# Attention and token/channel mixer on one core: left-over rows multiplied side by side, one load for q and k, a new order

## The chip, the cores and the metric

The kernel runs on one core of one Trainium2 chip, as one program. Its metric is the device time of one execution in microseconds (us). The core's engines run side by side, each on its own list of instructions: TensorE (PE in the profile, with PEld for its weight loads), VectorE (DVE), ScalarE (ACT), GpSimd (POOL) and SyncE (SP). They wait for each other by semaphores. DMAs are issued from the lists of SP and of ACT.

## The reference

Eight attention heads of 576 positions and 64 channels for a batch of 4 feed two mixing layers. All numbers are float32.

```python
scores = q @ k.T / sqrt(64) + bias[head, i, j]       # bias from a small network of log1p|i-j| / log1p(i)
attn = exp(scores - max); attn = attn / (sum(attn) + 1e-9)
x = (attn @ v) laid out as (batch, 576, 512)
u = x + (relu(x.T @ w_tok1) @ w_tok2).T              # mixing over the 576 positions, 256 inner
out = u + relu(u @ w_ch1) @ w_ch2                    # mixing over the 512 channels, 1536 inner
```

## The kernel before, in words

**Precision.** TensorE multiplies in pieces: an operand is split into a high part and the left-over low part, and high x high, high x low and low x high are summed in PSUM. So every product is three matmuls. q and k are split into rounded float32 parts (`kh`, `kl`, `qh`, `ql`), the softmax numerators, v, x and the weights into float16 parts.

**Units.** A unit is one batch entry and one pair of heads; there are 16 (`unit`). The 576 query rows of a unit are four chunks of 128 rows and 64 left-over rows. In the four chunks the two heads have separate score products, each over 64 contracted rows (the two heads lie in the two halves of the partitions). The left-over rows of both heads share one score product: head 0 in partitions 0 to 63, head 1 in 64 to 127.

**Steps of a chunk.** `scores` (PE, L792) writes a pair of PSUM banks; `biased` (DVE, L801) adds the bias and takes the row maximum; `numer` (ACT, L814) takes the exponential. Then 128x128 blocks of the numerators are turned so that keys lie on partitions: by TensorE (`flip`, L843), read out as high part by ACT (L846) and low part by DVE (L849); in chunks 0, 2 and the left-over chunk three of the blocks go by a DMA transpose, after ACT (L824) and POOL (L828, then L389) made the halves. `back` (PE, L870 to L872) multiplies the turned blocks by v, 30 matmuls a chunk, five blocks for each head; an extra column of ones in v gives the row sums.

**The left-over rows in `back`.** Turned block tiles hold 128 columns, of which a head owns 64. The kernel loads 128 columns from a place shifted by 64, so that the wanted rows land in the half of the partitions that the batch entry's parity asks for; the other half comes out as rubbish. For this the turned tiles have 64 extra columns at each end, which `fillt` (L619) sets to zero at the start. Both heads' results land in the same 64 partitions, in two column ranges.

**Normalisation.** After chunks 1 and 3, and again after the left-over rows, DVE adds a guard to the row sums (`norm1`, L891), takes reciprocals (`norm2`, L895) and multiplies (`norm3`, L904): nine instructions a unit. The result is `x`, of which ACT takes the high part (`xh`) and POOL the low part (`xl`).

**Token mixing of the unit.** `mix1` (L920 to L922) and `mix2` (L929 to L931) are 30 matmuls each. The left-over 64 positions are a fifth chunk, in the half of the partitions given by the parity; the weight tile `wt1` has two versions of its last chunk, one for each parity. The sum goes to DRAM (`um`, and `ul` for the left-over rows).

**Loads.** k and q of a unit come by one DMA each, issued from ACT's list (L750), into one buffer each (`kk`, `qq`). ACT rounds each (two activations, L374); POOL takes the low parts (L389; for the first unit DVE). The rounded tiles have two buffers.

**Order.** Nothing of the order is left to the compiler. `Plan` takes each step with a cost per engine, the steps it follows, the buffers it takes and frees, and a due time, and plays them forward: it always takes, on the engine that is free first, the step that is ready with the smallest due time. The due times are the table `DUE` plus the unit's place; `ON` has the costs where a step may go to several engines. The engines then run their lists in that order. Where the plan sees PE idle for long, it adds dummy matmuls (`keep_warm`, L323). The four single PSUM banks are shared by the flips, the mixing steps and the sums of `back` (two holds a unit).

**Around the units.** Ahead of them the bias is built (L521, four groups of 32 array columns side by side; L526; written to DRAM and read back); token weights are decoded from 64-bit words on DVE, POOL and ACT (L639 to L656). After them the channel mixing runs (L1111 to L1113, L1202 to L1204, L1296 to L1298).

Of the kernel before, what the change touches and what calls it, by code (L numbers as in the profile page):

```python
# [29 lines left out]
NCH = 4  # L30
# [9 lines left out]
STAY = 1486.1  # L40
# [16 lines left out]
ON = {'dlo': {'P': 1.9},  # L57
      'dlo2': {'P': (1.9, 1923.78), 'V': (0.67, 744.69)},
      'late': {'P': (0.7, 2192.22), 'A': (0.58, 2154.6)},
      'klow': {'P': (1.5, 404.86), 'V': (0.83, 1698.46)},  # L60
      'zlow': {'P': (1.25, -2022.79), 'V': (0.6, 1951.58)},
      'twhole': {'P': (2.4, -5410.44), 'V': (1.21, -163.47)},
      'tsum': {'P': (3.0, 1980.67), 'V': (1.72, -1127.53)},
      'tlow': {'P': (2.1, 1817.8), 'V': (1.15, 2280.4)},
      'oall': {'P': (2.7, 1683.65), 'V': (1.2, 3850.72)},
      'norm': {'V': (0.35, -2113.5), 'A': (0.88, -183.64)},
      'over': {'A': 0.65, 'V': (0.72, 599.08)},
      'vh': {'P': (0.7, 5073.08), 'V': (0.4, -2032.12), 'A': (0.6, -2896.69)},
      'vl': {'P': (1.36, 4039.97)}}
DUE = {'tie': 4736.26,  # L70
       'blk': -676.16,
       'blkn': 59.25,
       'rect': -364.19,
       'bmm': -2656.99,
       'over': -2660.88,
       'put': -3571.25,
       'bl': -179.13,
       'bln': 44.73,
       'sums': 1179.41,
       'sumsn': 532.92,  # L80
       'measw': 321.39,
       'measwn': 107.97,
       'amax': 767.52,
       'scales': 78.49,
       'scalet': -2778.06,
       'scalec': -884.57,
       'fill': -1967.61,
       'fill1': 321.78,
       'tok': -1836.05,
       'tokn': -264.96,  # L90
       'dec1': -196.68,
       'dec2': 362.43,
       'dec3': -442.95,
       'dec4': 845.97,
       'dec5': -898.57,
       'load_k': -385.67,
       'load_q': -829.68,
       'split_k': -303.52,
       'first_k': 1018.99,
       'first_q': -464.55,  # L100
       'split_q': -401.35,
       'load_v': -2691.07,
       'prep_v': 4811.82,
       'prep_vh': -1580.3,
       'prep_vl': -5129.6,
       'scores': -1550.06,
       'biased': -570.84,
       'exp': -803.8,
       'hi': -461.44,
       'lo': 874.4,  # L110
       'turn': -277.35,
       'flip': -1079.29,
       'fliphi': -883.4,
       'flip2': -920.66,
       'fliplo': 433.23,
       'back': 787.76,
       'norm': -94.44,
       'mix0': -1114.2,
       'mix1': 190.17,
       'relu': -3325.99,  # L120
       'mix2': -2565.13,
       'mix2b': -87.08,
       'store': -2250.33,
       'w1': 437.81,
       'w1n': 293.74,
       'U0': 957.44,
       'U0n': -427.31,
       'U1n': -290.77,
       'U1': 808.64,
       'U2': -710.17,  # L130
       'Un': 48.66,
       'U3': 2131.25,
       'U4': -678.33,
       'u1': 2779.66,
       'u2': -237.57,
       'u3': -558.34,
       'u4': -2241.32,
       'u5': -756.44,
       'G': 3117.15,
       'G0': 1449.33,  # L140
       'G0n': 0.0,
       'g1': -1447.72,
       'g2': 796.85,
       'ur': -324.62,
       'H': 2342.06,
       'e1': 448.66,
       'e2': -2521.07,
       'e3': 10.12,
       'e4': 1249.03,
       't2': 1665.81,  # L150
       't3': -678.77,
       't4': -818.53,
       'T1': -762.26,
       'Tn': -160.17,
       'rd': 479.45,
       'urs': -341.92,
       'un': 158.68,
# [1247 lines left out]
```

## Time and profile before

| | |
|---|---|
| time, three runs | 632.61, 632.66, 633.25 us (median 632.66) |
| the profiled execution | 629.27 us, its span 627.3 us |
| granted TensorE clock | 1.0 in the whole span |
| busy share of the span | PE 97%, DVE 77%, ACT 65%, POOL 48% |
| units | from about 57 us to about 345 us, the last store at 362 us |

The span is the time from the first to the last instruction; some 2 us of the execution lie around it. A matmul's record lasts longer than the time until the next one can start, because matmuls are pipelined: 128x65 products have records of 0.19 us and start 0.03 us apart. So a busy PE is not a full PE, and starts tell more than durations. Each engine runs its list strictly in order, so a late operand holds up all that is behind.

### The profile page before, as it was taken

Reading aid. Unit: us, or ns where it says so; the run is one execution under the profiler, and the core shown is the slowest. Engines: PE = TensorE matmul, PEld = TensorE weight load, DVE = VectorE, ACT = ScalarE, POOL = GpSimd, SP = SyncE. Lnnn points to the kernel's source line nnn. Section 1 sums busy time; section 2 is a strip of 40 time slices with the busy share of each in tenths; the row PEclk is TensorE's granted clock in tenths of the full one; section 3 lists DMA queues with packets and bytes.
Section 4 is the critical chain, followed back from the end, with each engine's and each line's share of the span. In section 5 each row is a group of like instructions: output and inputs, shape, how many; then the busy total and the mean of one; then the engine's idle time right before and its main releaser. Section 6 shows DMA issues by size and latency. Waiting matters only on the chain.

```text
span 627.3 us, 18135 instructions
## 1 busy us (share of the span) xinstructions
PE 607.8 (97%) x7216; PEld 446.8 (71%) x7216; DVE 484.5 (77%) x1220; ACT 407.3 (65%) x751; POOL 302.0 (48%) x343
## 2 busy tenths in 40 slices
PE   8999988999999999999999999999999999999997
PEld 4446776898898889889889964444444468845886
DVE  7887899889999899999899969985764784355322
ACT  7998889797888998998898434633543641244210
POOL 1006788976775888898564620002335642212211
PEclk9999999999999999999999999999999999999999
DMA  8999678999988966556856999645122015400221
GB/s 306 397 378 332 182 190 214 266 259 206 228 190 245 213 150 148 136 120 170 144 104 148 188 358 238 204 137 135 34 67 71 31 35 135 101 1 0 85 86 33
DMA packets 102340, 104.54 MB, mean 167 GB/s; under 512 B 62192, under 2 KB 71920, under 8 KB 102256
## 3 DMA queue, kind: packets, MB, share of 16 engines
q1 hardware_dynamic: 92608, 82.79, 50.5%
q10 hardware_dynamic: 9648, 20.60, 11.1%
q8 instruction: 56, 0.92, 0.6%
q14 instruction: 28, 0.23, 0.1%
HBM read 68.88 MB, written 20.33 MB: 142 GB/s over the span
## 4 chain that ended last, share of the span: by engine, by line
PE 66%; DVE 11%; ACT 8%; POOL 8%; issue 4%; DMA 2%; ACTq 0%; SPq 0%; POOLq 0%; DVEq 0%
PE bank L1111 5%; PE bank L1113 5%; PE bank L1112 5%; PE pair L792 5%; PE bank L1297 4%; PE bank L1296 4%; PE bank L1298 4%; PE pair L521 4%; PE bank L843 4%; DVE z L801 4%; DVE t2a L849 3%; PE pair L1113 2%; PE bank L1202 2%; PE pair L1111 2%; PE bank L1204 2%
## 5 line engine op out<-in xcount | busy, mean ns | idle before, releaser
L814 ACT ACTIVATE z<-z,mx 128x576 f32<-128x576 f32 (+1 forms) x121 | 92.6, 778 | 10.1 <-DVE mx L801 8.8
L801 DVE CUSTOM_DVE_ANT_0 z<-pair,slots 128x576 f32<-128x576 f32 (+1 forms) x121 | 90.6, 756 | 5.2 <-PE pair L792 4.5
L849 DVE SCALAR_TENSOR_TENSOR t2a<-bank,t2a 128x384 f16<-128x384 f32 (+1 forms) x134 | 70.6, 536 | 6.3 <-ACT t2a L846 5.0
L843 PE MATMUL bank<-id,z 128*128 128x128 f32 x431 | 71.0, 283 | 2.1 <-ACT z L814 0.7
L846 ACT ACTIVATE t2a<-bank 128x384 f16<-128x384 f32 (+1 forms) x134 | 62.3, 471 | 12.2 <-PE bank L843 8.3
L792 PE MATMUL pair<-kh,qh 64*128 64x288 f32 (+1 forms) x288 | 61.6, 345 | 4.1 <-DVE mx L801 3.3
L1111 PE MATMUL bank<-slots 128*128 128x512 f16 (+1 forms) x168 | 58.6, 349 | 0.0
L1113 PE MATMUL bank<-slots 128*128 128x512 f16 (+1 forms) x168 | 58.6, 349 | 0.0
L1112 PE MATMUL bank<-slots 128*128 128x512 f16 (+1 forms) x168 | 58.6, 349 | 0.0
L1307 DVE SCALAR_TENSOR_TENSOR slots<-bank,crow,slots 128x256 f32<-128x256 f32 x42 | 19.6, 481 | 47.6 <-PE bank L1298 34.1
L843 PEld LDWEIGHTS bank<-id,z 128*128 128x128 f32 x431 | 45.6, 141 | 12.3 <-DVE t2a L849 3.5
L870 PE MATMUL bank<-vh,t2a 128*128 128x65 f16 x472 | 53.5, 194 | 0.0
L871 PE MATMUL bank<-vl,t2a 128*128 128x64 f16 x472 | 53.2, 191 | 0.0
L872 PE MATMUL bank<-vh,t2a 128*128 128x65 f16 x472 | 53.2, 192 | 0.0
L792 PE MATMUL pair<-kl,qh 64*128 64x288 f32 (+1 forms) x288 | 51.9, 298 | 0.0
L792 PE MATMUL pair<-kh,ql 64*128 64x288 f32 (+1 forms) x288 | 50.4, 291 | 0.0
L1241 POOL TENSOR_TENSOR me<-me 128x512 f32<-128x512 f16 x12 | 13.7, 1154 | 68.8 <-DVE wd L1087 68.4
L792 PEld LDWEIGHTS pair<-kh,qh 64*128 64x128 f32 (+1 forms) x288 | 33.9, 184 | 16.0 <-issue 7.6
L871 PEld LDWEIGHTS <-t2a 128*128 128x128 f16 x472 | 43.6, 98 | 0.2
L870 PEld LDWEIGHTS <-t2a 128*128 128x128 f16 x472 | 43.4, 97 | 0.2
L872 PEld LDWEIGHTS <-t2a 128*128 128x128 f16 x472 | 43.5, 97 | 0.0
L870 PE MATMUL bank<-vh,rect 128*128 128x65 f16 x328 | 40.9, 195 | 2.3 <-DMA rect<-rect 1.5
(272 smaller groups left out, 2100.7 us busy)
## 6 DMA issues: line engine op xcount, KB each, us to landing
keep<-wc SPq DMA_DIRECT2D x24, 512.0 KB, 4.5
wd<-wc SPq DMA_DIRECT2D x24, 512.0 KB, 4.7
bd<-slots SPq DMA_DIRECT2D x36, 295.5 KB, 6.8
slots<-bd SPq DMA_DIRECT2D x16, 576.0 KB, 7.2
tv<-v ACTq DMA_DIRECT2D x16, 320.0 KB, 3.7
qq<-qT ACTq DMA_DIRECT2D x16, 320.0 KB, 3.7
kk<-kT ACTq DMA_DIRECT2D x16, 320.0 KB, 5.0
z<-vr SPq DMA_DIRECT2D x8, 576.0 KB, 7.7
```

The costliest lines, as they stand in the source:

```text
L792: PE.matmul(out=pairs[both[h].i][:, 512 - i + n * i:512 + n * i], lhsT=qx[x][w, c * 128:c * 128 + 128], rhs=kx[y][w, k0:k0 + i], start=(j ...
L801: V.tensor_tensor_reduce(out=st["z"][z.i][:, o], in0=pairs[ph.i][:, 512 - i:512 + i], in1=bias_m[hp][:, c, h, :] if c < NCH else bias_l[hp ...
L814: A.activation(out=zz, in_=zz, func=ACTF.Exp, bias=mx_t[z.i][:, h:h + 1], scale=-1.0)
L843: PE.transpose(banks[tb.i][:, n * 128:(n + 1) * 128], st["z"][z.i][:, 384 * i + n * 128:384 * i + (n + 1) * 128], id32)
L846: A.activation(out=block(h.i, 0, m), in_=banks[tb.i][:, 0:128 * m], func=ACTF.Copy, scale=P_SCALE)
L849: V.scalar_tensor_tensor(out=block(h.i, 3, m), in0=banks[tb.i][:, 0:128 * m], scalar=P_SCALE, in1=block(h.i, 0, m), op0=ALU.mult, op1=ALU. ...
L870: PE.matmul(out=o, lhsT=lh, rhs=vh[:, n, 0:D + 1], start=(i == 0), stop=False)
L871: PE.matmul(out=ps[:, h, 0:D], lhsT=lh, rhs=vl[:, n, :], start=False, stop=False)
L872: PE.matmul(out=o, lhsT=ll, rhs=vh[:, n, 0:D + 1], start=False, stop=(i == 4))
L1111: PE.matmul(out=ps, lhsT=w[0][:, c], rhs=uh[:, c], start=(c == 0), stop=False)
L1112: PE.matmul(out=ps, lhsT=w[0][:, c], rhs=ul[:, c], start=False, stop=False)
L1113: PE.matmul(out=ps, lhsT=w[1][:, c], rhs=uh[:, c], start=False, stop=(c == 3))
```

## The change

The left-over rows of the two heads are multiplied by v in two halves of the array's columns: head 0's 64 columns write partitions 0 to 63, head 1's write 64 to 127, one after the other in turn. The zero margins of the turned tiles, the shift by parity and the second version of the weights' last chunk go; `x` holds head 0's left-over rows in the upper left and head 1's in the lower right, zeros elsewhere; the last 64 columns of `wt2` are copied once so that the second product gives both halves. `norm1` and `norm2` run after chunk 1 (four columns) and after the left-over rows (five columns); the left-over rows are multiplied in two instructions of 64 rows (`norm4`). k and q come in one DMA and are rounded by one activation; the low parts stay two. The left-over store is two DMAs. `ON` gets an entry by which the low part for the DMA transpose could go to DVE (the built program never uses it). All due times have new values.

```diff
-STAY = 1486.1
+STAY = 1932.68
-       'back': 787.76,
+       'back': 1188.32,
-                 "kk": 1, "qq": 1, "kh": 2, "qh": 2, "tv": 1, ...
+                 "kq": 1, "gh": 2, "tv": 1, ...
-    tok = [(wt1[:, 0:2], 512), (wt1[:, 2:4], 512), (wt1[:, 4:6], 512),
+    tok = [(wt1[:, 0:2], 512), (wt1[:, 2:4], 512), (wt1[:, 4:5], 256),
-        fillt = add({"P": 2.6}, DUE["fill1"], lambda e: [G.memset(t[:, a:a + 64], 0.0) for t in st["t2a"] + st["t2d"] for a in (0, 832)], after=[drawn])
+        twice = add({"P": 0.6}, DUE["tok"] + DUE["tokn"] * 6, lambda e: [copy("P", w[:, :, S:640], w[:, :, 512:S]) for w in st["w2"]], after=wt_s[3:])
-            lk = add(wire("k", 1.06), t0 + DUE["load_k"], load("kk", hk, kT), after=early, take=[hk])
-            lq = add(wire("q", 1.06), t0 + DUE["load_q"], load("qq", hq, qT), after=early, take=[hq])
+            lk = add(wire("k", 2.0), t0 + DUE["load_k"], lambda e: ENG[e].dma_start(out=st["kq"][hk.i], in_=kq[order_of[u]]), after=early, take=[hk])
-                s = add({"A": 0.63}, t0 + DUE["split_" + nm], high(o, ho, x, hx), after=[ld], take=[ho])
+            high = add({"A": 1.18}, t0 + DUE["split_k"], lambda e: copy(e, st["gh"][gk.i][0], st["kq"][hk.i]), after=[lk], take=[gk])
...
-                            d = 64 * (h - b % 2) if c == NCH else 0
-                            lh, ll = (tt[t][:, y[t] + d:y[t] + d + 128] for y in (th, tl))
+                    if c < NCH:
+                        turns = [[(h, n + h, n, slice(0, 128), i)] for h in range(2) for i, n in enumerate(range(4 * h, 4 * h + 5))]
+                    else:
+                        turns = [[(0, n + 5 * h, n, slice(64 * h, 64 * h + 64), n) for h in range(2)] for n in range(5)]
+                    for turn in turns:
+                        for x, y, d in ((th, vh, D + 1), (th, vl, D), (tl, vh, D + 1)):
+                            for h, n, t, w, i in turn:
+                                PE.matmul(out=ps[w, h, 0:d], lhsT=tt[t][:, x[t] + w.start:x[t] + w.stop], rhs=y[:, n, 0:d], ...)
...
-                if c in (0, 2):
+                if c not in (1, NCH):
                     continue
+                hr, n = Hold("rc"), 4 if c == 1 else 5
+                main = norm3 if n == 4 else lambda e, f=norm3: f(e, c=2)
+                def norm4(e, hb=hb, hr=hr):
+                    for h in range(2):
+                        q = slice(64 * h, 64 * h + 64)
+                        xo, ps, rc = st["x"][xh_.i][q, 4, q], av_of(hb)[q, 2, 0, 0:D], rc_t[hr.i][q, 2, 0]
+                        ...
+                            V.tensor_scalar(out=xo, in0=ps, scalar1=rc, scalar2=None, op0=ALU.mult)
...
-                add(wire("store", 0.07), t + DUE["store"], lambda e: ENG[e].dma_start(out=u_l[b // 2][r, cs], in_=x()[r, 5]), after=[s8], free=[xh_])]
+                *(add(wire("store", 0.05), t + DUE["store"], lambda e, q=slice(64 * h, 64 * h + 64): ENG[e].dma_start(
+                    out=u_l[b // 2][r, hp * 128 + q.start:hp * 128 + q.stop], in_=x()[q, 5, q]), after=[s8], free=[xh_]) for h in range(2))]
```

On PE, the start of the left-over rows of the first unit, of before and then of the changed kernel. `rect` is a tile turned by DMA, `vh` and `vl` are the parts of v, and the numbers behind a name tell buffers apart.

```order
L843 MATMUL bank_66<-id_73,z_122 128x128 x3
L870 LDWEIGHTS rect
L870 MATMUL bank_68<-vh_111,rect 128x65
L871 LDWEIGHTS rect
L871 MATMUL bank_68<-vl_112,rect 128x64
L872 LDWEIGHTS rect
L872 MATMUL bank_68<-vh_111,rect 128x65
```

```order
L846 MATMUL bank_69<-id_73,z_116 128x128 x3
L874 LDWEIGHTS rect
L874 MATMUL bank_67<-vh_106,rect 64x65
L874 LDWEIGHTS rect
L874 MATMUL bank_67<-vh_106,rect 64x65
L874 LDWEIGHTS rect
L874 MATMUL bank_67<-vl_107,rect 64x64
L874 LDWEIGHTS rect
L874 MATMUL bank_67<-vl_107,rect 64x64
```

Thirty loads and thirty matmuls stay thirty; each now has 64 output rows instead of 128, and neighbours belong to the two heads.

On DVE, the end of a unit in the middle of the program, of before and of the changed kernel. `rc` holds the reciprocals, `x` the unit's result, `t2a` a turned tile.

```order
L895 RECIPROCAL rc_144<-rc_144 128x4
L849 SCALAR_TENSOR_TENSOR rect<-bank_69,rect 128x384
L801 ISA z_119,mx_138<-pair_64,slots 128x576
L801 ISA mx_138 128x1
L904 TENSOR_TENSOR x_85<-bank_67,rc_144 128x256
L801 ISA z_119,mx_138<-pair_65,slots 128x576
L801 ISA mx_138 128x1
L891 TENSOR_SCALAR rc_145<-bank_67 64x2
L849 SCALAR_TENSOR_TENSOR t2a_91<-bank_66,t2a_91 128x384
L895 RECIPROCAL rc_145<-rc_145 64x2
L904 TENSOR_TENSOR x_85<-bank_67,rc_145 64x128
```

```order
L885 TENSOR_SCALAR rc_139<-bank_66 128x5
L852 SCALAR_TENSOR_TENSOR rect<-bank_69,rect 128x384
L852 SCALAR_TENSOR_TENSOR t2a_91<-bank_68,t2a_91 128x384
L888 RECIPROCAL rc_139<-rc_139 128x5
L898 TENSOR_TENSOR x_83<-bank_66,rc_139 128x256
L912 TENSOR_SCALAR x_83<-bank_66,rc_139 64x64 x2
L852 SCALAR_TENSOR_TENSOR t2a_92<-bank_69,t2a_92 128x384
```

The 128x256 multiplication of chunks 2 and 3 stood ahead of the left-over rows' sums; it now stands behind them, with two 64x64 multiplications after it.

On ACT, the rounding of q and k of a unit in the middle, of before (k is rounded 18 rows further down) and of the changed kernel:

```order
L846 ACTIVATE t2a_90<-bank_67 128x384
L374 ACTIVATE qh_105<-qq 128x640
L814 ACTIVATE z_120<-z_120,mx_139 128x576
L374 ACTIVATE xh<-x_83 128x640
L824 ACTIVATE rect<-z_120 128x384
```

```order
L814 ACTIVATE z_113<-z_113,mx_132 128x576
L375 ACTIVATE kqh_102<-kq 128x1280
L945 ACTIVATE hh<-bank_68 128x256
L849 ACTIVATE t2a_94<-bank_66 128x384
L824 ACTIVATE rect<-z_113 128x384
```

One activation of 1280 columns stands where one of 640 stood, and the second one further down is gone.

## Rows read from the trace of the kernel before

**Rows 1.** The page: the span, busy time by engine, and the last chain's shares.

```profile
span 627.3 us, 18135 instructions
PE 607.8 (97%) x7216; PEld 446.8 (71%) x7216; DVE 484.5 (77%) x1220; ACT 407.3 (65%) x751; POOL 302.0 (48%) x343
...
PE 66%; DVE 11%; ACT 8%; POOL 8%; issue 4%; DMA 2%; ACTq 0%; SPq 0%; POOLq 0%; DVEq 0%
```

**Rows 2.** Windows: stretch, length, each engine's busy time, clock, DMA share, GB/s.

```profile
57.00:137.00 80.00, 72.64 (x1074) 63.16 (x1075) 73.62 (x206) 69.86 (x132) 64.93 (x100) 1.00 0.82 219
...
57.00:345.00 288.00, 276.35 (x4593) 247.30 (x4594) 264.83 (x726) 252.85 (x476) 217.41 (x261) 1.00 0.78 185
```

**Rows 3.** A window after the units, same columns.

```profile
380.00:420.00 40.00, 40.00 (x188) 18.21 (x187) 38.83 (x80) 23.30 (x37) 0.00 (x0) 1.00 0.69 184
```

**Rows 4.** Timeline of PE, one unit's left-over rows: first and next; then scores' start.

```profile
195.88 0.19 PE L870 MATMUL bank<-vh,rect 128*128 128x65 f16 x1
...
196.79 0.52 PE L843 MATMUL bank<-id,rect 128*128 128x128 f32 x3
...
200.39 0.19 PE L872 MATMUL bank<-vh,t2a 128*128 128x65 f16 x1
200.52 0.40 PE L792 MATMUL pair<-kh,qh 64*128 64x288 f32 x2
```

**Rows 5.** Narrow and wide arrays: timeline (PE, PEld), one group's mean between.

```profile
15.67 0.57 PE L521 MATMUL pair<-rect,slots 128*32 128x464 f32 x4
...
L521 PE MATMUL pair<-rect,slots 128*32 128x464 f32 x8 | 1.0, 552 | 0.0
...
5.96 0.21 PEld L521 LDWEIGHTS pair<-slots 128*32 128x32 f32 x12 [0.27 <-DVE slots L499]
...
341.45 0.31 PEld L843 LDWEIGHTS bank<-id,z 128*128 128x128 f32 x3 [0.17 <-DVE rect L849]
```

**Rows 6.** One line of the kernel: counts, then duration min/median/max in ns.

```profile
L374 ACT ACTIVATE qh<-qq x16: 720/736/762, 20.7 to 303.5; 128x640 fp32r<-128x640 f32 x16
L374 ACT ACTIVATE me<-me x6: 1056/1057/1057, 443.4 to 505.6; 128x1024 f16<-128x1024 f32 x6
L750 ACTq DMA_DIRECT2D qq<-qT x16: 334/335/370, 10.0 to 287.0; - x16
...
L951 SPq DMA_DIRECT2D ul<-x x16: 461/482/1569, 119.0 to 362.3; - x16
```

**Rows 7.** DVE groups by shape, 140 to 300 us: busy us, mean ns.

```profile
L904 DVE TENSOR_TENSOR x<-bank,rc 128x256 f32<-128x256 f32 x19 | 8.0, 420 | 0.3
...
L904 DVE TENSOR_TENSOR x<-bank,rc 64x128 f32<-64x128 f32 x9 | 2.6, 287 | 0.2
L895 DVE RECIPROCAL rc<-rc 64x2 f32<-64x2 f32 x9 | 1.4, 159 | 0.3
L891 DVE TENSOR_SCALAR rc<-bank 64x2 f32<-64x2 f32 x9 | 1.4, 153 | 0.2
```

**Rows 8.** The last chain's pieces on POOL at the units' start: start, us.

```profile
59.27 1.02 POOL t2a L619 x12
...
60.33 0.81 POOL rect L619 x9
...
106.69 1.09 POOL wt1l L389
```

**Rows 9.** DMA issues: KB each, median us to landing.

```profile
kk<-kT ACTq DMA_DIRECT2D x16, 320.0 KB, 5.0
...
z<-vr SPq DMA_DIRECT2D x8, 576.0 KB, 7.7
```

**Rows 10.** A wait in 60 to 345 us: total us, times, longest.

```profile
ACT xh L374 <- DVE x L904: 1.4, 6, 0.4
```

**Rows 11.** POOL groups by shape: busy us, mean ns.

```profile
L389 POOL TENSOR_TENSOR kl<-kk,kh 128x640 fp32r<-128x640 f32 x15 | 23.3, 1555 | 2.8 <-ACT kh L374 0.8 <-ACT z L814 0.7 <-issue 0.7
...
L647 POOL TENSOR_TENSOR keep<-keep 128x512 f32<-128x512 f32 x12 | 14.0, 1165 | 10.6 <-DVE keep L644 9.7 <-ACT t2a L846 1.0
```

More of the change, by code (lines that the diff above doesn't have):

```diff
@@ L70 @@
[L70 to L115, printed above, removed]
-       'back': 787.76,
[L117 to L157, printed above, removed]
-       'v1': 443.15,
-       'v2': 3631.75,
-       'v3': 1579.05,
-       'v4': 3836.34,
-       'v5': 958.72,
-       'v6': 674.78,
-       'v7': 160.67,
-       'v8': -1837.21,
-       'w2m': -1548.46,
-       'w2mn': 106.13}
@@ L690, in attention_mixer @@
         wt_s, plain_s = [], []
[L691 removed]
+        places = [slots[:, 3, 3674 + 512 * i:3674 + 512 * i + (512, 512, 256)[i]] for i in range(3)]
         places += [slots[:, 2, 8 * S + 288 * i:8 * S + 288 * i + 288] for i in range(2)] + [slots[:, 1, 8 * S + 288 * i:8 * S + 288 * i + 288] for i in range(2)]
@@ L874, in unit @@
-                backs.append(chain("back", add({"T": 0.917}, t + DUE["back"], back, after=[*turned_s, v3, *set_ok, *backs[-1:]], take=[hb, xh_] if c == 0 else [hb] if c == 2 else [],
+                    if c < NCH:
+                        turns = [[(h, n + h, n, slice(0, 128), i)] for h in range(2) for i, n in enumerate(range(4 * h, 4 * h + 5))]
+                    else:
+                        turns = [[(0, n + 5 * h, n, slice(64 * h, 64 * h + 64), n) for h in range(2)] for n in range(5)]
@@ new lines, in back @@
+                    for turn in turns:
+                        for x, y, d in ((th, vh, D + 1), (th, vl, D), (tl, vh, D + 1)):
+                            for h, n, t, w, i in turn:
+                                PE.matmul(out=ps[w, h, 0:d], lhsT=tt[t][:, x[t] + w.start:x[t] + w.stop], rhs=y[:, n, 0:d],
+                                          start=(i == 0 and x is th and y is vh), stop=(i == 4 and x is tl))
+                backs.append(chain("back", add({"T": 0.917 if c < NCH else 0.52}, t + DUE["back"], back, after=[*turned_s, v3, *set_ok, *backs[-1:]], take=[hb, xh_] if c == 0 else [hb] if c == 2 else [],
@@ L941, in unit @@
                 out=st["hh"][1], in0=p1(), scalar=0.0, in1=st["hh"][0], op0=ALU.max, op1=ALU.subtract), after=[s4], use=[b1])
-            s6 = chain("mix", add({"T": 1.7}, t + DUE["mix2"], mix2, after=[s5, *wt_s[3:]], take=[b2], free=[hh], use=[b1]))
+            s6 = chain("mix", add({"T": 1.7}, t + DUE["mix2"], mix2, after=[s5, *wt_s[3:], twice], take=[b2], free=[hh], use=[b1]))
             s7 = add({"V": 0.67}, t + DUE["mix2b"], lambda e: V.scalar_tensor_tensor(
```

253 lines of the change are left out of this document (169 added, 84 removed).

## The prediction

> **What bounds the kernel now.** I read the page's busy shares and its last chain first [rows 1], then windows by stage [rows 2, 3], then the lines that the change touches. The page calls PE 97% busy, which says little. After the units PE is busy 40 of 40 us, and the change gives it no less to do there [rows 3]; so what can move is the part up to about 343 us. The chain spends 66% of 627.3 us on PE, that is 414 us, of which some 284 lie after 343; 130 are left, 38% of the first 343 us. The 11% of DVE are 69 us, the 8% of ACT and of POOL 50 us each, nearly all of it ahead of 343: about 20%, 15% and 15% [rows 1]. In the units' stretch DVE is busy 265 of 288 us, ACT 253 without the time in which it issues DMAs, PE 276 by its long records [rows 2]. So no engine alone is the bound: the chain changes hands, and of a microsecond taken from one engine about its share of the chain should come through. I use 0.38 for PE, 0.20 for DVE, 0.15 for ACT. It is an estimate: an engine freed alone gives less, all freed together give more.
>
> **The left-over products (PE).** The thirty matmuls of a unit run from 195.88 to 196.79 us: 0.91 us, 30 ns from start to start, with nothing waiting in between [rows 4]. After the change they are fifteen pairs. Does the array run two column halves side by side? The bias stage answers for four groups of 32 columns: one 464-column matmul has a record of 0.55 us, and four of them, one for each group, took 0.57 us together [rows 5]. So streaming takes 15 x 30 ns = 0.46 us. The loads are less sure. The only loads of narrow arrays in the trace, twelve of 32 columns, took 0.21 us; one takes 0.11, so they follow each other 9 ns apart [rows 5]; twice as many columns would be 18 ns, and thirty loads 0.55 us. At the pace of full-width float32 loads, three in 0.31 us with 0.14 for one [from the same row: (0.31 - 0.14) / 2 = 85 ns for 128 columns], 64 columns would be 43 ns, and thirty in a row 1.28 us. I take 0.55, since that row is of column groups. Changing how the array is cut costs about 0.10: scores on two row halves start 0.13 us after the last product, against 0.03 otherwise [rows 4]. Together 0.65, bounds 0.46 and 1.48 (two changes). So 0.26 less a unit, between 0.45 less and 0.57 more; by sixteen units and 0.38: **-1.6 us**, bounds -2.7 and +3.5.
>
> The Trainium skill has a rule against this part. "TensorEngine Tiling (Array Packing)", section Tiling Modes, says that column tiling switches off fast weight load, and "TensorE: Matmul & The Clock Gate", section LDWEIGHTS, gives a load without it columns/1.2 ns. By that a 64-column load is an estimated 53 ns: 0.80 us for fifteen pairs side by side, 1.6 us in a row, and the term would be about 0 or +4.8 us. No run so far shows a float16 load of 64 columns.
>
> **q and k (ACT).** Two activations of 640 columns take 0.736 us each; 1024 columns take 1.057, so 0.84 ns a column, and 1280 columns 1.27 [rows 6]. That is 0.20 less; one DMA issue of 0.335 goes as well [rows 6]. 0.53 a unit, x 16 x 0.15: **-1.3 us**. The bounds are 0, if ACT only waits longer, and -8.5, if ACT were the bound throughout. Behind the long activation stand exponentials and read-outs, which may be 0.5 us later; that is the reason to stay at the chain's share. The DMA now brings 640 KB; the nearest row, 576 KB, lands after 7.7 us, against 5.0 for 320 KB [rows 9]. Nobody feels it while the loop of the one buffer fits a unit: 0.34 issue + 7.7 + 1.27 + two low parts of 1.56 on POOL [rows 11] = 12.4 us, against 288/16 = 18 us a unit. The cover is 5.6 us; without it scores of every unit would be late by the rest. The second left-over store costs SP 0.48 us a unit [rows 6]; a DMA transpose may stand behind it, but DMA is 2% of the chain [rows 1], so between 0 and 0.2 us: nothing.
>
> **Normalisation (DVE).** The group of the left-over rows goes: 153 + 159 + 287 ns = 0.60 us; a fifth column in the sums is counted at nothing, since with two columns these instructions already take 0.15 us. Two multiplications of 64x64 come: not shown; each is at least the 0.15 of a tiny tensor_scalar that reads PSUM and at most the 0.29 of 64x128 [rows 7]. I take 0.20, nearer to the tiny one, as half the 64x128's columns. So 0.20 less a unit, between 0.30 and 0.02; x 16 x 0.20: **-0.6 us**, bounds -4.8 (DVE the bound) and 0.
>
> **The start (POOL).** The memsets of the margins stand in the chain at 59 to 61 us with 1.02 + 0.81 us [rows 8]; they go. The third token part halves: of its POOL work the joining product, 1.17 us at full size [rows 11], and the last low part, 1.09 in the chain [rows 8], give back 0.55 each. The new copies of 64 columns come behind the last low part of the second weights, and the first unit's `mix2` now waits for them; between 0.2 us (two of the memsets) and 1.09, say 0.4. Net 2.5 us. DVE is busy 73.6 of 80 us in that stretch and POOL 64.9 [rows 2], so DVE is soon the next; I count two thirds: **-1.6 us**, bounds 0 and -2.5.
>
> **Sum.** -1.6 - 1.3 - 0.6 - 1.6 = -5.1 us. The profiled execution took 629.27 us, 2 us more than its span, so it would be 624.2. It is 3.4 us (0.5%) below the median of the runs shown; the same amount off the median 632.66 gives **627.6 us**. The new order is counted at nothing in this sum: on the places shown it only makes room for the new instructions.
>
> **Rivals.**
> *Narrow loads in a row.* Thirty loads of 64 columns, one after the other at the pace of float32 loads, hold a left-over group at 1.28 + 0.10 = 1.38 us: 0.47 more a unit, x 16 x 0.38 = +2.9; with the other -3.5 the sum is -0.6, **632.0 us**. For it: the only fast 30 ns pace in the trace is that of full 128-column loads [rows 4]. Against it: the 9 ns of the 32-column ones [rows 5]. The Trainium skill's rule above would, with loads in a row, put this case near 634, an estimate by its page's figure.
>
> *The unit's end gets longer (slower).* The multiplication of chunks 2 and 3 now stands behind the left-over rows' sums, and the bank that holds both stays taken until two more instructions are done. Before, 0.60 us of DVE lay between the last product and `x`; after, 0.15 + 0.16 + 0.42 + 2 x 0.20 = 1.13 [rows 7]. ACT's high part of `x`, POOL's low part, `mix1` and the next taker of the bank all wait that 0.53 us more. If it comes through in every unit, 8.5 us: -5.1 + 8.5 = +3.4, **636.0 us**. It decides from ten units of sixteen on (5.1/0.53). For it: ACT already waits for just this multiplication, 6 times in the units [rows 10]. Against it: only 1.4 us in all, 0.4 at the longest; mixing of a unit runs beside the next unit's scores.
>
> *The new order frees more.* In 57 to 137 us PE lacks 80 - 72.6 = 7.4 us even by its long records [rows 2], for POOL's and DVE's work comes late there. If the shorter start lets the first units close up and half of that goes, -3.7 more: **623.9 us**. For it: all due times are new. Against: DVE has 6.4 us of room there and no more.
>
> **Chances.** The sum as it stands 0.56; narrow loads in a row 0.12; the longer end 0.12; a freer order 0.20. The likeliest is 627.6, by itself between 624.5 and 630.5. The range takes in the freer order with ACT or PE nearer to the bound than its chain share (two times the shares of PE and ACT, -2.9 more than 623.9, is 621.0) and most of the slow case: 620.5 to 634.5. What this measurement can tell from no change is about 0.2%, 1.3 us: faster means below 631.4, slower above 633.9. Of the first case 0.53 is faster, all of the freer order, 0.04 of the narrow loads; slower are 0.10 of the longer end and 0.03 of the narrow loads. So 0.77 faster, 0.10 the same, 0.13 slower.
>
> **What would show it.** In the changed trace: the left-over group on PE in 0.5 to 0.7 us from first to next start (right), 0.9 (no gain) or 1.3 and more (loads in a row); a rounding activation near 1.27 us; 64x64 multiplications near 0.2; units that end 3 to 5 us earlier relative to 57 us, with the stretch after them unchanged; ACT's wait for the multiplication before `xh` not above some 3 us in all. Wrong would be: PE idle behind the normalisation in most units, scores waiting for low parts of q and k, or a stretch after the units that has changed by more than a microsecond.

## The result, and the profile after

The changed kernel takes 636.1 us (median), the kernel before 632.8 beside it: a ratio of 1.0068, 95% interval 1.0053 to 1.0084. So the change is slower by 0.7%, 4.3 us, where 5.1 us less was forecast. Run once more among the experiments, it came out at 1.0055 (1.0028 to 1.0081).

The page of the changed kernel, profiled at 636.24 us: the span, the engines' busy times, the granted clock in 40 slices, and the last chain's shares.

```profile
span 634.5 us, 18086 instructions
PE 610.0 (96%) x7216; PEld 444.8 (70%) x7216; DVE 478.8 (75%) x1204; ACT 405.8 (64%) x735; POOL 297.5 (47%) x321
...
PEclk9999899999999889999999999999999999999999
...
PE 72%; DMA 7%; DVE 7%; ACT 6%; POOL 3%; issue 3%; SPq 1%; ACTq 0%; DVEq 0%; POOLq 0%
```

Against [rows 1], DVE has 6 us less to do, ACT 1.5, POOL 4.5, and yet the span is longer. DMA went from 2% of the chain to 7%, and the clock has two dips that the page of before does not have. The first of them (0.66 over 65 to 70 us) is absent in other runs of the same order and is left aside.

First the parts, on the engines where they act. The left-over rows of a unit on PE's timeline (the two columns in front are start and length), then the first scores:

```profile
161.59 0.22 PE L874 MATMUL bank<-vh,rect 128*64 128x65 f16 x2
161.64 0.20 PE L874 MATMUL bank<-vl,rect 128*64 128x64 f16 x2
...
162.06 0.20 PE L874 MATMUL bank<-vh,t2a 128*64 128x65 f16 x2
162.18 0.60 PE L792 MATMUL pair<-kqh 64*128 64x288 f32 x2
```

Fifteen pairs start 33 ns apart and 0.59 us pass until the scores, against 0.91 from the first product to the next matmul in [rows 4]. So two loads and two matmuls of 64 columns go where one of 128 went. The prediction quoted a rule of the Trainium skill against this: "TensorEngine Tiling (Array Packing)" says that column tiling switches off fast weight load (the rule stands in section Tile-to-Partition Mapping, Restrictions, not in Tiling Modes). With the estimate of 53 ns a load by the formula of "TensorE: Matmul & The Clock Gate", section LDWEIGHTS, a group would take at least 0.80 us; the measured 0.59 decides against it.

DVE's normalisation by shape in 140 to 300 us (busy us, mean ns of one, idle before), to be held against [rows 7]:

```profile
L898 DVE TENSOR_TENSOR x<-bank,rc 128x256 f32<-128x256 f32 x18 | 7.6, 421 | 0.4
L912 DVE TENSOR_SCALAR x<-bank,rc 64x64 f32<-64x64 f32 x18 | 5.0, 280 | 0.1
L888 DVE RECIPROCAL rc<-rc 128x5 f32<-128x5 f32 x9 | 1.7, 184 | 0.1
...
L885 DVE TENSOR_SCALAR rc<-bank 128x5 f32<-128x5 f32 x9 | 1.4, 159 | 5.7 <-PE bank L874 5.7
```

ACT's rounding of q and k as one, in 60 to 345 us, and the load's issues (KB each, median us to landing):

```profile
L375 ACT ACTIVATE kqh<-kq 128x1280 fp32r<-128x1280 f32 x15 | 19.0, 1267 | 0.7 <-PE pair L792 0.7
...
kq<-kq ACTq DMA_DIRECT2D x16, 640.0 KB, 5.1
```

The rounding takes 1.27 us as forecast. A 64x64 multiplication takes 0.28 us, not 0.20, so DVE saves only 0.03 us a unit.

The loss that can be seen stands near 215 us. SP's list of the changed kernel there, with the six bias loads of the last head pair (L725, L728):

```profile
197.33 2.33 SPq L725 DMA_DIRECT2D slots<-bd  x4
199.77 1.11 SPq L728 DMA_DIRECT2D slots<-bd  x2
201.34 7.69 SPq L835 DMA_TRANSPOSE rect<-rect  x2
```

The same place in the kernel before:

```profile
194.82 1.24 SPq L832 DMA_TRANSPOSE rect<-rect  x1
196.11 2.33 SPq L725 DMA_DIRECT2D slots<-bd  x4
198.54 1.11 SPq L728 DMA_DIRECT2D slots<-bd  x2
200.34 0.35 SPq L370 DMA_DIRECT2D keep<-wc  x1
203.39 1.31 SPq L832 DMA_TRANSPOSE rect<-rect  x1
```

Before, a DMA transpose stands ahead of the 2.6 MB (4 x 576 + 2 x 144 KB) and the next one 5 us behind. Their times to landing, in this order:

```profile
DMA to landing us min/median/max: 2.7/2.7/2.7
...
DMA to landing us min/median/max: 9.9/9.9/9.9
```

So the burst made a transpose slow before the change too, but PE did not need that tile sooner. ACT had issued q and v there (320 KB each) at 198.96 and 200.28, ahead of the transpose. Now a transpose stands directly behind the burst, and v (320 KB, issued on ACT at 202.65) and the new 640 KB of q and k (204.43) come behind it and run beside it. What happens to that tile, by the chain of waits (start, length, what), by PE's wait for it (total, times, longest) and by windows (PE, PEld, DVE, ACT, POOL busy, then clock, DMA share, GB/s):

```profile
201.34 17.80 DMA rect<-rect
...
219.19 1.03 PE bank L874 x30
```

```profile
PE bank L874 <- DMA rect<-rect: 5.7, 1, 5.7
```

```profile
200.00:205.00 5.00, 5.00 (x93) 4.37 (x93) 4.83 (x16) 4.83 (x10) 3.90 (x4) 1.00 1.04 394
205.00:210.00 5.00, 5.00 (x72) 4.41 (x71) 4.66 (x14) 4.45 (x10) 4.24 (x5) 1.00 1.40 137
210.00:215.00 5.00, 3.48 (x61) 3.33 (x58) 4.55 (x12) 3.55 (x6) 2.24 (x4) 1.00 1.02 101
215.00:220.00 5.00, 0.81 (x30) 0.82 (x30) 0.00 (x0) 0.00 (x0) 2.52 (x3) 0.87 1.16 207
220.00:225.00 5.00, 5.00 (x57) 4.33 (x53) 4.04 (x12) 3.69 (x6) 2.71 (x3) 0.50 0.55 144
225.00:230.00 5.00, 5.00 (x86) 4.78 (x84) 2.88 (x8) 3.55 (x7) 4.90 (x6) 0.94 0.15 53
```

The tile lands after 17.8 us. The DMA engines are busy all the while; they move 394 GB/s until 205 us and then, in 205 to 215, only 137 and 101. PE, DVE and ACT stand still, PE for 5.7 us, and then PE goes on at the granted clock 0.50, the lower of its two levels (1.2 GHz), in 220 to 225 us. The left-over scores of each unit, a mark that both kernels have, show it: DVE reads out the ninth at 212.8 us in both, the tenth at 237.6 against 232.3 before.

```profile
237.61 0.82 DVE L801 CUSTOM_DVE_ANT_0 z<-pair,slots 128x640 f32<-128x640 f32 x1
...
232.26 0.81 DVE L801 CUSTOM_DVE_ANT_0 z<-pair,slots 128x640 f32<-128x640 f32 x1
```

The second thing to see: at the ninth unit the changed kernel is not ahead at all, though the sum had half of its gain by then. The experiments take up both.

The third is one of the prediction's own signs of being wrong, a changed stretch after the units. From the sixteenth left-over scores to PE's first matmul with the second channel weights, before and then in the changed kernel:

```profile
338.51 0.81 DVE L801 CUSTOM_DVE_ANT_0 z<-pair,slots 128x640 f32<-128x640 f32 x1
400.30 0.38 PE L1202 MATMUL bank<-me,slots 128*128 128x512 f16 x1
...
343.30 0.81 DVE L801 CUSTOM_DVE_ANT_0 z<-pair,slots 128x640 f32<-128x640 f32 x1
406.95 0.38 PE L1209 MATMUL bank<-me,slots 128*128 128x512 f16 x1
```

That is 61.8 us before and 63.7 now, 1.9 more. Leaving out exchanged tables and doubled work, every trace below that runs in the new order has 63.6 to 64.8 us here, every one in the old order 61.6 to 62.8.

### The profile page after: what moved, and what is told of

Same layout as the page of the kernel before. It is cut to its first block, busy times and chain, and to the rows that moved or that the text cites. A ratio compares the mean times of both kernels' runs of the same rounds, so it can differ in the third digit from the quotient of the medians.

```text
span 634.5 us, 18086 instructions
## 1 busy us (share of the span) xinstructions
PE 610.0 (96%) x7216; PEld 444.8 (70%) x7216; DVE 478.8 (75%) x1204; ACT 405.8 (64%) x735; POOL 297.5 (47%) x321
## 4 chain that ended last, share of the span: by engine, by line
PE 72%; DMA 7%; DVE 7%; ACT 6%; POOL 3%; issue 3%; SPq 1%; ACTq 0%; DVEq 0%; POOLq 0%
PE pair L792 7%; PE bank L874 6%; PE bank L846 6%; PE bank L1119 5%; PE bank L1120 5%; PE bank L1118 5%; PE bank L1303 4%; PE bank L1304 4%; PE bank L1305 4%; PE pair L521 3%; DMA rect<-rect 3%; PE pair L1120 2%; PE pair L1118 2%; PE bank L1209 2%; PE bank L1211 2%
## 5 line engine op out<-in xcount | busy, mean ns | idle before, releaser
L849 ACT ACTIVATE t2a<-bank 128x384 f16<-128x384 f32 (+1 forms) x134 | 62.8, 470 | 16.4 <-PE bank L846 12.8
L792 PE MATMUL pair<-kqh 64*128 64x288 f32 (+1 forms) x288 | 62.8, 347 | 2.3 <-DVE mx L801 2.2
L874 PE MATMUL bank<-vh,t2a 128*128 128x65 f16 (+1 forms) x944 | 56.5, 196 | 0.0
L390 POOL TENSOR_TENSOR kql<-kq,kqh 128x640 fp32r<-128x640 f32 x30 | 46.3, 1555 | 14.8 <-ACT kqh L375 8.5
L792 PE MATMUL pair<-kql,kqh 64*128 64x288 f32 (+1 forms) x288 | 53.1, 301 | 0.0
L792 PE MATMUL pair<-kqh,kql 64*128 64x288 f32 (+1 forms) x288 | 51.4, 294 | 0.0
L874 PE MATMUL bank<-vl,t2a 128*128 128x64 f16 (+1 forms) x472 | 50.7, 194 | 0.0
L874 PEld LDWEIGHTS <-t2a 128*128 128x128 f16 (+1 forms) x1416 | 49.3, 101 | 1.4 <-issue 0.8
L874 PE MATMUL bank<-vh,rect 128*128 128x65 f16 (+1 forms) x656 | 41.6, 197 | 5.9 <-DMA rect<-rect 5.7
L792 PEld LDWEIGHTS pair<-kqh 64*128 64x128 f32 (+1 forms) x288 | 35.1, 186 | 13.8 <-issue 6.9
L874 PEld LDWEIGHTS <-rect 128*128 128x128 f16 (+1 forms) x984 | 33.8, 103 | 10.1 <-DMA rect<-rect 5.8
```

The source lines that it names most:

```text
L390: ENG[e].tensor_tensor(out=o, in0=x, in1=y, op=ALU.subtract)
L792: PE.matmul(out=pairs[both[h].i][:, 512 - i + n * i:512 + n * i], lhsT=g[x][w, KW + c * 128:KW + c * 128 + 128], rhs=g[y][w, k0:k0 + i], s ...
L849: A.activation(out=block(h.i, 0, m), in_=banks[tb.i][:, 0:128 * m], func=ACTF.Copy, scale=P_SCALE)
L874: PE.matmul(out=ps[w, h, 0:d], lhsT=tt[t][:, x[t] + w.start:x[t] + w.stop], rhs=y[:, n, 0:d], start=(i == 0 and x is th and y is vh), stop ...
```

## The experiments

All ratios are to the kernel before, run beside them. The first four tested the theory of the late tile (1) against costs of the parts (2), the size of the load (3) and the order as a whole (4).

**Spread loads** (`e1_spread`), in the finished list of steps:

```diff
+        held = [s for s in made if s.tag == ("bias", 3)]
...
+                if i >= on and s.tag and s.tag[0] == "turn" and held:
+                    made.append(held.pop(0))
```

Expected: 

> The changed kernel, with one thing moved: the six bias loads of the last head pair, which stand together directly ahead of a DMA transpose, are put one by one behind the next six transposes. Theory 1 (a transposed tile that is queued behind the 2.6 MB of bias loads comes 10 us late, PE idles 5.7 us for it and then runs 6.8 us at half clock): the wait for the tile near 202 us goes, 5.7 us of idle and some 3.4 us of half clock with it; part of such a gain was regained later anyway, so 628 to 631 us. Theory 2 (the changed products and normalisation cost more on their engines than thought): no change, 636. Theory 3 (the 640 KB load of q and k in one is what holds the transposes up): the tile stays late, 634 to 636.

Measured: 1.011 (1.0088 to 1.0131), a miss. Its waits in 195 to 240 us tell why:

```profile
DVE z L806 <- DMA slots<-bd: 7.3, 2, 5.1
```

The transposes land within 6.2 us and PE's wait is gone, but the last bias loads are now issued up to 230 us and DVE waits 7.3 us for them. One wait was exchanged for another.

**Before, with the loads ahead of a transpose** (`e2_before_behind`): the six steps are moved directly ahead of the next transpose.

Expected: 

> The kernel before, with its six bias loads of the last head pair moved from behind one DMA transpose to directly ahead of the next. Theory 1: the transposed tile behind them comes late (over 12 us from issue to landing instead of under 5), PE waits some 5 us near 210 us and may fall to the lower clock; 637 to 641 us against 632.8. Theories 2 and 3: the parts of the change are absent, so no change, 632 to 634.

Measured: 1.0004 (0.998 to 1.0028). A miss for theory 1: the transpose behind the loads landed after 10.4 us, and no wait came of it. That is hardly later than the 9.9 us which the kernel before has anyway, so the burst alone is not enough. In that kernel q, k and v come in pieces of 320 KB; q and v are issued during the burst and none in the 5 us behind it.

```profile
DMA to landing us min/median/max: 10.4/10.4/10.4
```

**The tables exchanged** (`e3_old_tables`, `e4_new_tables`): `DUE`, `ON` and `STAY` of one kernel in the other.

Expected: 

> The changed kernel's work in an order made by the old numbers (the due times, the costs of the free choices and the stay value of before; the low part for the DMA transpose on POOL as before). Theory 1 and 4 (the parts save the 5 us that the prediction sums up, and the new order takes them back): 627 to 630 us. Theory 2 (the parts themselves cost): 635 to 637. If the parts save nothing and cost nothing: 633.

Expected: 

> The kernel before, its work unchanged, in an order made by the new numbers. Theory 4 (the new numbers make a worse order, whatever the work): 638 to 643 us. Theory 1: slower only if a transposed tile that PE soon needs again stands right behind the bias loads of the last head pair; two transposes stand a few rows behind them here, so 634 to 640, with a wait of PE for a tile that came by DMA near 200 us. Theory 2: 632 to 634, as the changed parts are absent.

Measured: 1.0359 (1.0321 to 1.0398) and 1.0432 (1.040 to 1.0464), both outside every forecast. Each set of numbers fits its own work only, so the exchange says nothing of the parts; it shows that an order can easily cost 20 us.

**One, two, three** (`e5_one_two_three`): as the first, but one load behind the next transpose, two behind the second, three behind the third.

Expected: 

> As the first experiment, but the six bias loads stand sooner: one behind the next DMA transpose, two behind the second and three behind the third, so that the last is issued near 215 us instead of 230. Theory 1, as it stands now (two waits are near: PE's for a transposed tile behind the burst, DVE's for bias that comes too late): neither occurs, the 5.7 us of idle and 3.4 us of half clock near 215 us are saved and not spent elsewhere: 8 to 9 us less than the changed kernel, a ratio of 0.992 to 0.998 to the kernel before. Theory 5 (the stall costs nothing in the end, because what stands ahead of the later stages is late anyway): the ratio stays at 1.005 to 1.009.

**q and k later** (`e6_kq_later`): only the load of q and k next to the burst moves, behind the second transpose.

```diff
+        made.remove(kq_)
+        on = [i for i in range(at_, len(made)) if made[i].tag and made[i].tag[0] == "turn"][1]
+        made.insert(on + 1, kq_)
```

Expected: 

> The changed kernel, bias loads where it has them; only the one 640 KB load of q and k that is issued 3 us behind the burst (at 204 us) is issued behind the second DMA transpose, some 4 us later. Theory 3 (960 KB of v, q and k on the other queue beside the transposes make both slow: the DMA engines moved only some 50 KB a microsecond there): the tile lands within 12 us instead of 17.8, PE waits under 2 us, ratio 0.995 to 1.001. Theory 1 (the burst ahead of it is enough): the tile still lands after 15 us or more and the time stays at a ratio of 1.005 to 1.009.

Measured: 0.9992 (0.9972 to 1.0011) and 1.0009 (0.9983 to 1.0036). Either edit takes the loss away, 3 to 5 us (some 2 us of uncertainty, as the sets differ). The first is outside both of its forecasts: the gain of 8 to 9 us did not come. The second is close to theory 3: with q and k later the tile lands after 12.6 us, and PE waits 0.5 us for it:

```profile
PE bank L881 <- DMA rect<-rect: 0.5, 1, 0.5
```

So neither the burst nor the 640 KB is guilty alone: the transpose was late because it stood behind the one and beside the other. That settles the loss; the forecast gain was still missing. In the units it is there: in the trace of "one, two, three" the sixteenth left-over scores come at 334.85 us, 3.7 sooner than before. But the stretch behind them takes 64.3 us, and the two kernels end within 0.2 us of each other (spans 627.5 and 627.3).

**Products one head after the other** (`e7_serial`):

```diff
-                        turns = [[(0, n + 5 * h, n, slice(64 * h, 64 * h + 64), n) for h in range(2)] for n in range(5)]
+                        turns = [[(0, n + 5 * h, n, slice(64 * h, 64 * h + 64), n)] for h in range(2) for n in range(5)]
```

Expected: 

> The changed kernel with the left-over products of head 0 all ahead of those of head 1, instead of in turn: the same thirty loads and matmuls, no two of the array's halves side by side. Prediction's own reading: a group then takes 30 x 30 ns = 0.90 us or more instead of 0.59, 0.31 x 16 x 0.38 = +1.9 us or more against the changed kernel (ratio to before 1.009 to 1.014). Theory 2 (working side by side gains nothing, loads set the pace): the group stays at 0.59 and the time too (1.005 to 1.009).

Measured: 1.0092 (1.0062 to 1.0122), some 2 us over the changed kernel, not separable from it. (In its trace the late tile landed after 15.2 us and PE waited 2.7, so a shorter stall may hide part of the cost.) On the timeline the group takes 0.97 us from first start to the scores instead of 0.59:

```profile
161.30 0.22 PE L874 MATMUL bank<-vh,rect 128*64 128x65 f16 x1
...
162.27 0.40 PE L792 MATMUL pair<-kqh 64*128 64x288 f32 x2
```

The fifteen matmuls of each half still start 33 ns apart, but the first half's run until 161.77 us and the second half's from 161.68, almost one behind the other. (The 0.09 us between are starts out of the list's order, so for the two halves PE does not keep that order to the last matmul.) It is the turn-taking that makes the halves work at once.

**Work doubled**, to weigh an engine: the rounding (`e8_round_twice`, on the changed kernel), the 64x64 multiplications (`e11_norm4_twice`) and the left-over products (`e12_products_twice`), both on the kernel of "one, two, three".

Expected: 

> The changed kernel with each unit's rounding of q and k done twice: 1.27 us more of ACT a unit, 20.3 us in all. It measures the prediction's weight: by ACT's chain share of 0.15 it costs 3.0 us (ratio to before 1.010 to 1.013). If ACT is at the bound in the units it costs 10 us or more (over 1.020); if ACT has room to spare, under 1 us (1.005 to 1.009). By the same weight the 0.53 us a unit that the change takes from ACT are worth 1.3 us, seven or more, or nothing.

Expected: 

> The fifth experiment's kernel with the two 64x64 multiplications of each unit's left-over rows done twice: 0.56 us more of DVE a unit, 9 us in all, on the way from the last product to x. By the prediction's weight of 0.20 for DVE: +1.8 us on the fifth (ratio 1.001 to 1.003). By the rival of the longer end, each unit later by 0.56: +9 us (1.012 to 1.015). If DVE has room: no change (0.998 to 1.000).

Expected: 

> The fifth experiment's kernel with each unit's left-over products issued twice (the second pass writes the sums anew): 0.47 to 0.5 us more of PE a unit, 7.5 to 8 us in all. By the prediction's weight of 0.38 for PE: +3 us on the fifth (ratio 1.003 to 1.005). If PE is the bound throughout, since behind the units it has no idle time to give back: +7.5 us (1.010 to 1.013). If the units' waits hide it: under 1 us (0.998 to 1.001).

Measured: 1.0268 (1.0234 to 1.0302), 1.0092 (1.0068 to 1.0116), 1.0089 (1.0062 to 1.0117). Over their bases (for the first the mean of the changed kernel's two ratios, 1.0062) that is some 13 us of 20.3 on ACT, 6.3 of 9.0 on DVE and 6.1 of 7.9 on PE (15 pairs x 33 ns x 16): weights of 0.6 to 0.8, not the chain's 0.15, 0.20 and 0.38. The first may be too low: in its trace PE waits 1.5 us for a transposed tile instead of 5.7, so part of the stall is gone from its base. Over a base without the stall it would be some 17 us, a weight of 0.8.

**q and k apart again** (`e10_q_and_k_apart`): two loads and two roundings at the places of the one, on the same base.

Expected: 

> The fifth experiment's kernel with q and k loaded by two DMAs of 320 KB and rounded by two activations of 640 columns, as before the change, at the places where the one load and the one rounding stand: 0.20 us more of activation and one DMA issue of 0.33 a unit, 8.5 us of ACT in all. It measures what that part of the change is worth. By the prediction's weight of 0.15: +1.3 us on the fifth (ratio 1.000 to 1.002). By the weight that the doubled rounding showed, about 0.5: +4 to 5 us (1.005 to 1.008). If the part is worth nothing: the fifth's 0.999.

Measured: 1.003 (1.0003 to 1.0056): 2.4 us more than its base, with some 2 us of uncertainty. The part is worth about what the prediction gave it or a little more. Here 8.5 us of added work cost 2.4, a weight of 0.3 and not 0.6 to 0.8.

**Waits behind the units** (`e9_waits_out`). Waits of PE in 310 to 400 us of the changed kernel (total, times, longest), where the kernel before has 0.2 in all:

```profile
PE bank L1119 <- DMA slots<-slots: 0.9, 1, 0.9
PE bank L846 <- DVE rect L852: 0.8, 1, 0.8
PE bank L846 <- DVE t2a L852: 0.6, 2, 0.4
PE bank L351 <- ACT dgc L350: 0.5, 1, 0.5
```

The first has the second left-over store in its chain:

```profile
342.25 0.47 SPq L957
...
342.77 0.59 SPq L957
...
343.41 1.26 SPq L1102
...
344.72 2.54 DMA slots<-slots
...
347.30 0.28 PE bank L1119
```

Expected: 

> The changed kernel with the spread bias loads of the fifth experiment and the later load of q and k of the sixth, and with two waits of PE behind the units taken out: the left-over stores of two late units stand behind the transposes of u that the first channel products wait for (PE waited 0.6 to 1.2 us there), and the two small PE steps on the maximum of the second channel weights stand one step later each in PE's list (1.1 us there). Theory 6 (without the stall the units end 3 to 4 us sooner than before's, and it is PE's waits behind them, absent before the change, that give it back): 1.5 to 2 us less than the fifth experiment, ratio to before 0.994 to 0.998. Theory 5 (the second half is bound by the DMA loop of the weights, about 2 us a load, and waits only move on): no gain over the fifth, 0.998 to 1.001.

Measured: 1.0008 (0.999 to 1.0026). The two waits went and others came: 1.8 us for a DVE step of the first channel product, which stood in DVE's list behind the decoding of the second channel weights, and that behind their load. Its units end where those of the kernel before do (338.45 us against 338.51), and its stretch behind them takes 64.6 us against 61.8. So these two waits are not what makes the stretch longer, or not alone.

Then the parts, but for q and k and the token weights' third part, were put into the old order, each step at its old place (`e13_old_order`; `e15_old_order_memsets` keeps the memsets; `e14_after_again` is the changed kernel once more).

Expected: 

> The kernel before in its own order, instruction by instruction, with these parts of the change put in at their old places: the left-over products of the two heads in turn, the normalisation in two steps (five columns after the left-over rows, two 64x64 multiplications), no margins and no memsets of them, two left-over stores. q and k stay apart, and so do the token weights' third part and the old numbers of the order. Theory 4 (the parts are worth what the prediction gave them, -1.6 on PE, -0.6 on DVE, -1.2 of the start's 1.6, and the new order gives it back): 3 to 4 us less than before, ratio 0.993 to 0.996. Theory 7 (the parts are worth nothing in any order): 0.998 to 1.002. If the longer way from the last product to x costs more than the products save: above 1.003.

Expected: 

> The changed kernel itself, beside the two others of this set. All theories: a ratio to before of 1.005 to 1.009, with the wait for the late transposed tile near 215 us and the lower clock behind it.

Expected: 

> As the run in the old order, but with the memsets of the margins kept at the start (their columns are no longer read). What it is slower than that run is what the memsets cost. The prediction's step: 1.83 us of POOL in the last chain, two thirds of it through, 1.2 us, so a ratio 0.002 above the other. If the start has room: the same ratio within 0.001.

Measured: 1.0055 (1.0032 to 1.0079), 1.0055 (1.0028 to 1.0081; its tile landed after 16.5 us, PE waited 4.4), and 1.0059 (1.0037 to 1.0081). This ended theory 4 as it stood: without any new order these parts make the kernel slower by 3.5 us, so they have no net gain that the new order could take back. The memsets are worth 0.3 us by the pair, about 2 either way; in the traces the first left-over scores come no later with them (69.6 us) than without (70.0). ACT's wait for the last multiplication ahead of `xh` is 4.8 us in this run, against 1.4 in [rows 10]:

```profile
ACT xh L374 <- DVE x L902: 4.8, 9, 0.8
```

DVE's timeline of before and of this run at the same place of a unit shows one thing that the later place does:

```profile
173.37 0.66 DVE L364 TENSOR_REDUCE m<-keep 128x1 f32<-128x512 f32 x1
173.95 0.42 DVE L904 TENSOR_TENSOR x<-bank,rc 128x256 f32<-128x256 f32 x1
174.45 0.42 DVE L940 SCALAR_TENSOR_TENSOR hl<-bank,hh 128x256 f16<-128x256 f32 x1
```

```profile
177.23 0.68 DVE L364 TENSOR_REDUCE m<-keep 128x1 f32<-128x512 f32 x1
178.46 0.42 DVE L941 SCALAR_TENSOR_TENSOR hl<-bank,hh 128x256 f16<-128x256 f32 x1 [0.55 <-ACT hh L940]
```

Here the 128x256 multiplication used to fill a hole in which DVE would have waited for ACT. Behind the left-over rows it stands where DVE is wanted, and the hole stays empty.

The last three runs take the parts apart: `e16_one_multiplication` (it leaves out that head 1's left-over rows go to columns of their own), `e17_early_norm` (it leaves out the guard for the left-over rows), and `e18_before_late_norm`, which is the kernel before with

```diff
+                    if c == 3:
+                        return
```

in its normalisation, so that chunks 2 and 3 are done together with the left-over rows.

Expected: 

> The run in the old order, but with the normalisation as before the change: the 128x256 multiplication at its old place, then sums, reciprocals and a single multiplication of 128x64 for the left-over rows (it leaves out that head 1's rows go to their own 64 columns). What is left of the change is the products, the memsets and the second store. Theory 8 (the longer end of the unit costs, and the products gain on PE, 4.3 us of which PE, nearly always at work, passes on most): ratio 0.993 to 0.997. Theory 7 (the products gain nothing): 0.999 to 1.002. If the products themselves cost: above 1.003.

Expected: 

> The run in the old order with the 128x256 multiplication of chunks 2 and 3 back at its old place; for the left-over rows a reciprocal read straight from the sums (the guard of 1e-9 is left out there) and the two 64x64 multiplications. From the last product to x it is 0.16 + 0.56 = 0.72 us, against 0.60 before the change and 1.31 in that run. Theory 8: most of the products' gain is kept, ratio 0.995 to 0.999, and 3 us or more less than the run in the old order. Theory 7: 1.000 to 1.003. If it is the two short instructions that cost and not the place: 1.004 to 1.006.

Expected: 

> The kernel before with one thing changed: the sums, reciprocals and the 128x256 multiplication of chunks 2 and 3 stand behind the left-over rows' sums, as in the changed kernel (six columns at once, so DVE does 0.29 us less a unit). From the last product to x it is 1.04 us instead of 0.60. Theory 8 (the rival of the longer end): 0.44 us a unit later, 7 us by its own reckoning, some of it hidden and 4.6 us of DVE saved: 1.003 to 1.009. Theory 9 (DVE's time counts, not the place): 0.992 to 0.997.

Measured: 0.9974 (0.9956 to 0.9992), 0.9997 (0.9979 to 1.0015), 1.0021 (1.0001 to 1.0042). The products, with the memsets gone and the second store, gain 1.6 us (0.5 to 2.8). The two 64x64 multiplications in place of one cost 1.5 of these (0.9997 - 0.9974, not sure by itself). The later place costs another 3.7 (1.0055 - 0.9997, about 1.9 either way). By itself in the kernel before it costs 1.3 us (0.1 to 2.6), less than theory 8 said, although DVE then does 4.6 us less (16 x 0.29): theory 9 falls, it is the place that counts. With the long multiplication at its old place the wait ahead of `xh` is back where it was:

```profile
ACT xh L374 <- DVE x L903: 1.0, 3, 0.4
```

The hole shown above is not the whole reason. In 60 to 345 us DVE's waits for `hh` are 3.5 us before, 4.4 with the later place and 4.2 with the old place again. What does fall with the old place is ACT's wait for `x` (4.8 to 1.0), DVE's waits for ACT's read-outs of turned blocks (7.3 to 4.6) and DVE's for scores (5.7 to 3.5). Which of them PE feels is not shown.

No version with the full computation is faster than the kernel before beyond its interval.

## Why the prediction was wrong, step by step

- **Products on PE: right.** 0.59 us against 0.65 forecast; in the old order -1.6 us (0.5 to 2.8), the very term, though so close a hit is luck.
- **q and k on ACT: about right** in size (1.27 us, one issue less; worth some 2.4 +- 2 us, forecast 1.3). **"Nobody feels it" failed.** The load of 640 KB was compared with the time a unit takes, and its median of 5.1 us is better than the 7.7 assumed. Not compared was what else is under way in its worst moment: there it took 14.7 us and held up a transpose that PE needed.
- **"A DMA transpose may stand behind it ... nothing", and "the new order is counted at nothing": the steps that failed with the most weight.** DMA's 2% of the chain is a mean; the order moved one transpose behind the bias burst. 5.7 us of idle and the clock at 0.50 behind it cost 3 to 5 us by the two edits that take them away. The order of SP around the two bursts was there to be read. The new order's second price is the stretch after the units: the prediction wanted it unchanged, and it is 1.9 us longer.
- **Normalisation on DVE: wrong in sign.** As busy time it was -0.6 us; a multiplication was mis-sized (0.28 for 0.20), which leaves 0. The place costs more than the time: in the old order, place and shape together 5.1 us (1.0055 - 0.9974). This is the rival of the longer end, given 0.12 for 636.0 us. Its mechanism was found; its reckoning of 0.53 us a unit passed straight on is too high, as some of it is hidden. That its 636.0 meets the measured 636.1 is luck: it knew neither of the late tile nor of the longer stretch. How much of the later place the new order hides was not separated: there ACT waits only 0.9 us in all for the 64x64 multiplications, but doubling them still cost 6.3 us.
- **The start on POOL: not borne out, not ruled out.** -1.6 us were given; the memsets, 1.2 of it, are worth 0.3 us (about 2 either way) by the pair of runs in the old order. An early lead was not kept: the changed kernel was 5.9 us ahead at the third unit and 0.9 behind at the fifth. What took it back was not looked for.
- **The weights.** A chain share turned removed work into time tolerably (products 1.6 of 5.1 us), but the three runs with doubled work cost two to four times the share or more. The rounding and load of q and k in two, also added work, cost 0.3. So no one weight fits, and which work costs more than its share was not forecast.

The account: products -1.6, q and k -2.4, normalisation between 0 and +5, the late tile +3 to 5, the stretch behind the units about +2 by the traces; that makes +1 to +8, and the measured +4.3 lies within. It is no proof of the sum, as the parts were measured in different orders. How much of the normalisation the new order lets through, and which of PE's waits behind the units (2.8 us in 310 to 400 us, against 0.2 before) make the stretch longer, stays open.

## What to carry to other kernels

In a list order that fits closely, ask of every moved instruction which hole it leaves and what stands where it lands. In this kernel removed PE work returned a third of its time, and doubled work cost 0.6 to 0.8 of it; a chain's share does not tell the two apart. Look up what is queued ahead of each transfer that an engine waits for, and what runs on the other queue at that moment, not its median. An order made by tuned numbers belongs to one program: judge the parts of a change in a fixed order first.

## What the runs showed of the hardware that was not expected

A DMA transpose of a 128x768 float16 tile, 2.7 us to landing ahead of the burst, took 10.4 us behind 2.6 MB of loads on its own queue, 12.6 with v (320 KB) on the other queue beside it, and 15.2 to 17.8 in three traces with q and k as well (960 KB); the engines' busy share then was over 1.0 at 101 to 137 GB/s, against 394 in the 5 us before. Two 64-column halves of the array took a load and a matmul each within 33 ns when neighbours in PE's list belonged to different halves; when they did not, each half kept its 33 ns but the halves worked one after the other (0.97 us for the thirty instead of 0.59, both up to the scores). After 5.7 us without work PE was granted 0.50 of its clock in 220 to 225 us; after 4.4 us without work (the changed kernel run again) it was granted 0.68 and 0.64 in 215 to 225.
